# GpSimd in program order, and a step of attention reordered, in a kernel of attention and routed experts

## The chip, the cores and the metric

The kernel runs on one core of a Trainium2 chip, as one launch. The metric is the device time of the launch in microseconds: the median of the runs of the kernel before is 896.27 us (three runs, 895.25 to 897.72).

## The reference

Attention over 8 batches, 12 heads, 448 positions and a head size of 64, with capped scores, then a layer of 8 experts with a fixed capacity:

```
scores = cap*tanh(q@k.T/sqrt(64)/cap);  scores -= max;  attn = exp(scores);  attn /= sum + 1e-9
x = (attn@v) as rows of 768;  logits = x@w_gate
all (token, expert) pairs in order of falling logit: take a pair if the token is free and the expert has under 448 tokens
out[tokens of e] = relu(x@w1[e])@w2[e]
```

All inputs and the output are float32. There are 3584 tokens.

## The kernel before, in words

There are two stages. The first is attention (`attention`); the second routes the tokens and runs the experts (`Routing`, `ffn_all`). Everything that changes is in the first.

**A step.** The loop `for g in range(N)` has 24 steps. Step g takes four heads of one batch: b, m = divmod(g, 3), so a batch has a first, a second and a third step (m = 0, 1, 2). Two pairs of heads lie one above the other in the 128 partitions. In step g the program issues:

- `qk(g,r)`, r = 0 to 6: PE multiplies 64 keys by all queries into a PSUM tile of two banks (psS, two buffers), and ScalarE takes the tanh. After the second, the fourth and the seventh it has a group of tiles together and takes their exponential (line 154). From g = 3 on the first two exponentials are held back by one tanh.
- `avq(g-1,r)`: PE multiplies the values of the step before by its exponentials into two banks named psA. The seven parts are interleaved with those of `qk`.
- `esum`: VectorE adds the exponentials to `es`, for the denominators: e1 (the first two groups, right after the second exponential), and in the next step e2, r6 and in some steps r0.
- `tr(g+1,0)`, `tr(g+1,1)`: VectorE transposes k and q of the next step in blocks of 32.
- `av_out`: VectorE copies psA, one copy for each bank, to `xT`. The tile psA has two buffers of one bank.

**Work for earlier batches.** With bb = b-1, `rnd(bb,..)` multiplies `xT` by the gate weights and `es` by columns of ones on PE. In a third step `logit_in` copies that to SBUF, `sums` transposes the denominators and takes their reciprocals, and GpSimd copies them to `R32`. At the end of the third step `logit` transposes the logits on PE (four matmuls, line 240), scales them on VectorE (lines 245 to 253), and GpSimd adds over heads (line 257). In the first step of every other batch `on_logits` runs `propose_a` on VectorE (twelve small instructions, lines 462 to 473) and `propose_b` on GpSimd. `turn(b-2,p)` handles one pair of the batch two before: VectorE transposes it in blocks (x32, two buffers), GpSimd scales it (`xw`, line 229), and after two of them SP stores the result to `xs` in DRAM (line 233).

**What sets the order.** `manual_schedule` keeps PE, ScalarE, VectorE and SP in the order in which the program is written. GpSimd is not in its list, and a planner orders GpSimd's instructions. Each engine executes its own queue in order. The two PSUM pools here have 2 banks (pM, tiles psM: gate and sum results, logits) and 2 banks (pT, tiles psA); psS has 4.

Of the kernel before, what the change touches and what calls it, by code (L numbers as in the profile page):

```python
# [6 lines left out]
F32=mybir.dt.float32; F32R=mybir.dt.float32r; BF16=mybir.dt.bfloat16; F16=mybir.dt.float16; I32=mybir.dt.int32; I16=mybir.dt.int16  # L7
# [10 lines left out]
def attention(nc, tc, c1, xp, pM, q, k, v, cap, w_gate, xs, L1, ident, on_logits, on_turn, NDEF, setup, mark):  # L18
# [3 lines left out]
    B,H,S,D=q.shape  # L22
    CP=112; NJ=S//CP; NP=H//2; NQ=NP//2; E=w_gate.shape[1]; HG=2
    N=B*NQ
# [20 lines left out]
            if p==NP-1: nc.sync.dma_start(xs[b*S:(b+1)*S].rearrange("(j p) d -> p j d",j=NJ),xn[b])  # L45
        return rest
    with ExitStack() as ctx:
        ctx.enter_context(tc.manual_schedule(engines={mybir.EngineType.PE,mybir.EngineType.Activation,mybir.EngineType.DVE,mybir.EngineType.SP}))
        nat=ctx.enter_context(tc.tile_pool(name="nat",bufs=3))
        tp=ctx.enter_context(tc.tile_pool(name="tp",bufs=2))  # L50
        ep=ctx.enter_context(tc.tile_pool(name="ep",bufs=2))
# [5 lines left out]
        NB=S//32  # L57
# [99 lines left out]
        def esum(g,what):  # L157
# [13 lines left out]
            else:  # L171
                r=int(what[1])
                add(t[:,0],t[:,0],ev(g,r) if r else t[:,1])
        avp={}
        def avq(g,r):
            if not 0<=g<N: return
            if r==0:
                for o in range(2): avp[g,o]=pM.tile([128,512],F32,name="psM") if g==N-1 and not o else pT.tile([128,512],F32,name="psA")
            if g:
                z=nats[g,2]  # L180
                for o in range(2):
                    hp=slice(o*64,o*64+64)
                    for h in range(2):
                        nc.tensor.matmul(avp[g,o][h*64:h*64+64,:S],z[hp,r,h,:],ev(g,r)[hp,h,:],start=r==0,stop=r==6)  # L184
                return
            j,x=(r%3,r//3) if r<6 else (3,1)
            z,zh=nats[g,2]
            for w in range(2):
                o=w^x; hp=slice(w*64,w*64+64)
                for h in range(2):  # L190
                    lhs,rhs=(z[hp,j,HG*h+o,:],ex(g,o,j)) if j<3 else (zh[hp,h,:],ev(g,6))
                    nc.tensor.matmul(avp[g,o][h*64:h*64+64,:S],lhs,rhs[hp,h,:],start=(j==0 and x==0),stop=j==3)
        def av_out(g,o):
            if not 0<=g<N: return
            b,m=divmod(g,NQ)
            if m==0 and o==0: xT[b]=xp.tile([128,NP,S],F32,name="xT",bufs=3)
            nc.vector.tensor_copy(xT[b][:,2*m+o,:],avp[g,o][:,:S])  # L197
        def rnd(b,*ns,of=None):
            of=of or (ROUNDS if b else FIRST)
            for n in ns:  # L200
# [17 lines left out]
            for x in range(4): nc.gpsimd.tensor_copy(R32[b][32*x:32*x+32],rec[64+32*(x//2):96+32*(x//2)])  # L218
        def stored():
            while stores: stores.pop(0)()  # L220
        def turn(b,p):
            stored()
            if not 0<=b<B-NDEF: return
            t=xp.tile([128,S],F32,name="x32",bufs=2)
            nc.vector.transpose(t,xT[b][:,p,:])
            m,o=divmod(p,2); r=(0,2,1,3,4,5)[p]
            if not o: xw[0]=xp.tile([128,NB,32,2],F32,name="xw",bufs=2)
            w=xw[0]
            nc.gpsimd.tensor_tensor(w[:,:,:,o],t.rearrange("p (k i) -> p k i",i=32),R32[b][:,:,r:r+1].broadcast_to([128,NB,32]),op=ALU.mult)
            def store():  # L230
                for x in range(4):
                    c=m*256+x*64
                    nc.sync.dma_start(xs[b*S:(b+1)*S,c:c+64].rearrange("(k q) d -> q k d",q=32),w[32*x:32*x+32].rearrange("p k i o -> p k (i o)"))
            if o: stores.append(store)
        def logit(b,what=0,part=None,pool=None):
            p0=64 if what==2 else 0; W=128-p0
            lg=lgs.pop(b)
            ps=pool.tile([128,512],F32,name="psA") if pool else pM.tile([128,512],F32,name="psM")
            for j in range(NJ):
                mark[0]=nc.tensor.transpose(ps[:CP,j*W:(j+1)*W],lg[p0:,j*CP:(j+1)*CP],ident[p0:,p0:])  # L240
            va=ps[:CP,:NJ*W].rearrange("p (j c) -> p j c",j=NJ)
            if b not in rin: rin[b]=xp.tile([CP,NJ,H],F32,name="rin",bufs=2)
            r=rin[b]
# [10 lines left out]
                    r[:,:,8:12].unsqueeze(3).broadcast_to([CP,NJ,4,E]),op=ALU.mult)  # L254
            if what!=1:
                if b<B-NDEF:
                    add=lambda o,x,y: nc.gpsimd.tensor_tensor(o,x,y,op=ALU.add)
                    add(t[:,:,0:6],t[:,:,0:6],t[:,:,6:12])
                    add(t[:,:,0:3],t[:,:,0:3],t[:,:,3:6])
                    add(t[:,:,0:1],t[:,:,0:1],t[:,:,1:2])  # L260
                    add(L1[:,b*NJ:(b+1)*NJ,:].unsqueeze(2),t[:,:,0:1],t[:,:,2:3])
                else: nc.vector.tensor_reduce(L1[:,b*NJ:(b+1)*NJ,:],t.rearrange("p j s e -> p j e s"),axis=AX.X,op=ALU.add)
# [808 lines left out]
```

## Time and profile before

| what | value |
|---|---|
| median of three runs | 896.27 us |
| profiled execution, its own time | 895.05 us |
| its span | 893.1 us |
| PE busy | 854.5 us, 96% |
| VectorE (DVE) busy | 594.6 us, 67% |
| ScalarE (ACT) busy | 574.5 us, 64% |
| GpSimd (POOL) busy | 418.1 us, 47% |
| mean granted clock of TensorE | 0.994 |

The span is from the first to the last instruction of the program; the execution's own time is 1.95 us longer. A line such as "L149 ACT" names the line of the kernel and the engine. In a timeline the first column is the start in us, the second the duration of the instructions that were merged into the line, xN their number, and the bracket the idle time of the engine before them and what ended it. A PE line counts each matmul of this kernel twice or more, since float32 takes several passes.

### The profile page before, as it was taken

The page shows a single profiled execution, that of the slowest core. Times are in us where ns is not written, and L with a number is a line of the kernel's source. Part 1 is how long each engine was busy: PE and PEld are TensorE (multiplying, and loading weights), DVE is VectorE, ACT ScalarE, POOL GpSimd, SP SyncE. Part 2 cuts the span into 40 slices and gives each one's busy share as a digit, 9 for nine tenths or more (in the row PEclk, how much of TensorE's full clock was granted, in tenths as well). Part 3 has the DMA queues.
Part 4 walks back from the last instruction along what each step waited for, and adds up shares of the span by engine and source line. Part 5 has one row for each costly group of instructions (what it writes and reads, how often), then busy time and mean ns, then how long its engine had stood idle before and what let it go on. Part 6 is the DMA issues. An engine that isn't in the chain of part 4 may idle for free.

```text
span 893.1 us, 17659 instructions
## 1 busy us (share of the span) xinstructions
PE 854.5 (96%) x6092; PEld 621.4 (70%) x6092; DVE 594.6 (67%) x1967; ACT 574.5 (64%) x813; POOL 418.1 (47%) x626
## 2 busy tenths in 40 slices
PE   6999998998999898899999999999999999999997
PEld 3333333333333336888988989989989989999997
DVE  3778887888787988866777777777767773130210
ACT  6899996987989775256374573673754745425521
POOL 8102121213031214356465585593784765856941
PEclk9999999999999999999999999999999999999999
DMA  8899999598885311470760882864936927928701
GB/s 119 131 144 150 156 148 171 98 167 123 141 124 94 70 35 63 150 244 17 226 181 19 232 264 78 239 215 144 275 112 194 280 84 189 312 61 233 240 10 54
DMA packets 363385, 133.70 MB, mean 150 GB/s; under 512 B 290624, under 2 KB 356160, under 8 KB 363296
## 3 DMA queue, kind: packets, MB, share of 16 engines
q1 hardware_dynamic: 353792, 102.27, 54.6%
q0 software_dynamic: 4656, 22.02, 7.2%
q10 hardware_dynamic: 4848, 8.29, 2.9%
q8 instruction: 48, 0.79, 0.4%
q14 instruction: 41, 0.34, 0.1%
HBM read 94.40 MB, written 30.08 MB: 139 GB/s over the span
## 4 chain that ended last, share of the span: by engine, by line
PE 63%; DVE 10%; issue 9%; DMA 5%; SPq 5%; ACT 4%; POOL 4%; POOLq 0%; DVEq 0%; ACTq 0%
PE psH L914 23%; PE psH L945 19%; PE psA L184 9%; PE psS L138 7%; DVE es L160 3%; SPq L85 2%; DMA k<-in_k_dram 2%; ACT e L149 2%; PE psM L206 2%; ACT e L154 2%; DMA xg<-xs,idx 1%; DVE xT L197 1%; DVE cmpD L527 1%; POOL out_dram L927 1%; POOL w2l L796 1%
## 5 line engine op out<-in xcount | busy, mean ns | idle before, releaser
L945 PE MATMUL psH<-w2h,hh 128*128 128x384 f32 x896 | 235.3, 340 | 0.0
L149 ACT ACTIVATE e<-psS 128x896 f32<-128x896 f32 x168 | 148.2, 913 | 39.1 <-PE psS L138 34.5
L945 PE MATMUL psH<-w2l,hh 128*128 128x384 f32 x512 | 166.5, 340 | 0.3 <-POOL gap L794 0.2
L138 PE MATMUL psS<-tq,tk 64*64 64x448 f32 x1288 | 152.0, 549 | 11.1 <-DVE tq L123 5.6
L945 PEld LDWEIGHTS psH<-w2h,hh 128*128 128x128 f32 x896 | 161.8, 188 | 0.3
L184 PE MATMUL psA<-e,nv 64*64 64x448 f32 x1260 | 147.2, 547 | 10.1 <-DVE xT L197 10.1
L154 ACT ACTIVATE e<-e,bias 128x1792 f32<-128x1792 f32 (+2 forms) x74 | 147.2, 1991 | 1.0
L914 PE MATMUL psH<-xgh,w1h 128*128 128x448 f32 x384 | 143.1, 373 | 0.3 <-ACT xgh L874 0.3
L914 PE MATMUL psH<-xgh,w1l 128*128 128x448 f32 x384 | 141.4, 368 | 0.0
L914 PE MATMUL psH<-xgl,w1h 128*128 128x448 f32 x384 | 136.8, 369 | 0.0
L796 POOL TENSOR_TENSOR w2l<-w2r,w2h 128x768 fp32r<-128x768 f32 x64 | 118.1, 1846 | 37.7 <-ACT w2h L792 26.9
L796 POOL TENSOR_TENSOR w1l<-w1r,w1h 128x768 fp32r<-128x768 f32 x62 | 114.3, 1845 | 19.2 <-ACT w1h L792 14.9
L138 PEld LDWEIGHTS psS<-tq,tk 64*64 64x64 f32 x1288 | 50.1, 133 | 92.7 <-issue 45.4
L184 PEld LDWEIGHTS psA<-e,nv 64*64 64x64 f32 x1260 | 53.4, 135 | 80.7 <-issue 55.6
L945 PEld LDWEIGHTS psH<-w2l,hh 128*128 128x128 f32 x512 | 95.6, 188 | 1.3 <-POOL gap L794 1.2
L920 ACT ACTIVATE hh<-psH 128x448 fp32r<-128x448 f32 x64 | 34.8, 544 | 86.1 <-PE psH L914 79.8
L922 DVE SCALAR_TENSOR_TENSOR hh<-psH,hh 128x64 fp32r<-128x64 f32 (+1 forms) x128 | 43.9, 385 | 67.4 <-ACT hh L920 66.3
L951 ACT ACTIVATE on<-psH 128x384 f32<-128x384 f32 x48 | 23.4, 487 | 88.5 <-PE psH L945 82.5
L160 DVE TENSOR_TENSOR es<-es,e 128x896 f32<-128x896 f32 (+2 forms) x51 | 77.2, 1513 | 1.4 <-ACT e L154 0.3
L914 PEld LDWEIGHTS psH<-xgh,w1h 128*128 128x128 f32 x384 | 72.5, 189 | 5.6 <-ACT xgh L874 0.5
L914 PEld LDWEIGHTS psH<-xgh,w1l 128*128 128x128 f32 x384 | 72.3, 188 | 5.2
L914 PEld LDWEIGHTS psH<-xgl,w1h 128*128 128x128 f32 x384 | 72.2, 189 | 5.0
(368 smaller groups left out, 1269.2 us busy)
## 6 DMA issues: line engine op xcount, KB each, us to landing
w1r<-in_moe_w_dram SPq DMA_DIRECT2D x128, 192.0 KB, 4.6
w2r<-in_moe_w_dram SPq DMA_DIRECT2D x64, 384.0 KB, 6.0
k<-in_k_dram SPq DMA_DIRECT2D x92, 112.0 KB, 3.8
q<-in_q_dram SPq DMA_DIRECT2D x92, 112.0 KB, 4.0
nv<-in_v_dram SPq DMA_DIRECT2D x92, 112.0 KB, 3.2
xs<-xw SPq DMA_DIRECT2D x72, 112.0 KB, 2.5
xz<-pl ACTq DMA_DIRECT2D x18, 384.0 KB, 3.1
xs<-xn SPq DMA_DIRECT2D x2, 1344.0 KB, 6.2
```

The lines of the kernel that those rows point to most:

```text
L85: (nc.scalar if first and a else nc.sync).dma_start(z[w:w+32,lo*NB:hi*NB,:],src[b,h0+2*t+lo:h0+2*t+hi,:,a*32:a*32+32].rearrange("h (k s) d ...
L138: nc.tensor.matmul(ps[o*64:o*64+64,h,:S],tks[g,0][hp,o,r*64:r*64+64],tks[g,1][hp,o,:],start=True,stop=True)
L149: nc.scalar.activation(ev(g,r),ps[:,:,:S],AF.Tanh,scale=sr[0])
L154: act=lambda: nc.scalar.activation(e,e,AF.Exp,scale=sr[1],bias=bias)
L160: t=es_t[g]; add=lambda o,a,b: nc.vector.tensor_tensor(o,a,b,op=ALU.add)
L184: nc.tensor.matmul(avp[g,o][h*64:h*64+64,:S],z[hp,r,h,:],ev(g,r)[hp,h,:],start=r==0,stop=r==6)
L796: (eng or nc.gpsimd).tensor_tensor(view(l),r,view(h).bitcast(F32),op=ALU.subtract)
L914: nc.tensor.matmul(ps[:,:C],a[:,c,:],b[:,c,:],start=(m==0),stop=(m==DC*3-1)); m+=1
L920: nc.scalar.activation(h[:,:C],ps[:,:C],AF.Relu)
L922: nc.vector.scalar_tensor_tensor(h[:,d:d+b-a],ps[:,a:b],0.0,h[:,a:b].bitcast(F32),op0=ALU.max,op1=ALU.subtract)
L945: nc.tensor.matmul(ps[:,:HD],h[:,f,a:a+128],spl[p,2,hf,f//2][w][:,f%2,:],start=(m==0),stop=(m==nm-1))
L951: if t<3: nc.scalar.activation(ons[p][0][:,t*DM+hf*HD:t*DM+hf*HD+HD],ps[:,:HD],AF.Copy)
```

## The change

1. GpSimd is added to the list of `manual_schedule`: its instructions run in program order.
2. psA becomes one tile of two banks with one buffer. `av_out(g)` is one copy of both banks, and it is issued at the start of step g+2, ahead of the first `avq`, and no longer at the end of step g+1. The last step keeps two tiles (`alast`) and two copies.
3. `turn(b,m)` takes both pairs of a step in one transpose and one scaling (x32 with one buffer of twice the size), at the start of the step, behind `av_out` and `heads` and ahead of both block transposes `tr`. Before there were two, at two places in the step.
4. From g = 3 on both block transposes stand together ahead of `esum`.
5. `logit` is split: `ltr` (PE's transposes) in the middle of the next first step, the rest at the end of that step, the sums over heads (`heads`, GpSimd) at the start of the second step, `on_logits` at the end of the second step.
6. `logit_in` and `sums` go from the middle of the third step to its end, behind e1. In the last third step (g = 23) `logit_in` and `logit` stay in the middle.

```diff
-        ctx.enter_context(tc.manual_schedule(engines={mybir.EngineType.PE,mybir.EngineType.Activation,mybir.EngineType.DVE,mybir.EngineType.SP}))
+        ctx.enter_context(tc.manual_schedule(engines={mybir.EngineType.PE,mybir.EngineType.Activation,mybir.EngineType.DVE,mybir.EngineType.Pool,mybir.EngineType.SP}))
...
+                two=None if g==N-1 else pT.tile([128,2,512],F32,name="psA",bufs=1)
+                for o in range(2): avp[g,o]=(alast(o) if two is None else two[:,o])
+                pair[0]=two
...
+            if g<N-1: nc.vector.tensor_copy(xT[b][:,2*m:2*m+2,:],pair[0][:,:,:S])
+            else:
+                for o in range(2): nc.vector.tensor_copy(xT[b][:,2*m+o,:],avp[g,o][:,:S])
...
+        def turn(b,m):
             if not 0<=b<B-NDEF: return
+            t=xp.tile([128,2,S],F32,name="x32",bufs=1)
+            nc.vector.transpose(t.rearrange("p o s -> p (o s)"),xT[b][:,2*m:2*m+2,:].rearrange("p o s -> p (o s)"))
+            w=xp.tile([128,NB,32,2],F32,name="xw",bufs=2)
+            r=R32[b][:,:,m:m+3:2] if m<2 else R32[b][:,:,4:6]
+            nc.gpsimd.tensor_tensor(w.rearrange("p k i o -> p k o i"),t.rearrange("p o (k i) -> p k o i",i=32),r.unsqueeze(3).broadcast_to([128,NB,2,32]),op=ALU.mult)
...
+        def heads(b):
+            if b not in lts: return
+            t=lts.pop(b)
+            add=lambda o,x,y: nc.gpsimd.tensor_tensor(o,x,y,op=ALU.add)
+            add(t[:,:,0:6],t[:,:,0:6],t[:,:,6:12])
+            add(t[:,:,0:3],t[:,:,0:3],t[:,:,3:6])
+            add(t[:,:,0:1],t[:,:,0:1],t[:,:,1:2])
+            add(L1[:,b*NJ:(b+1)*NJ,:].unsqueeze(2),t[:,:,0:1],t[:,:,2:3])
...
             order=g>=G2; first=bb==0
+            av_out(g-2)
+            if m==0 and bb>1: on_turn(bb-2)
             for j in range(2 if order else 3): avq(g-1,j)
-            turn(b-2,2*m)
+            stored()
+            if m==1: heads(bb-1)
+            turn(b-2,m)
             tr(g+1,0)
+            if order: tr(g+1,1)
             for w in ('e2','r') if g==1 else ('e2','r6','r0'): esum(g-1,w)
             qk(g,2)
             if order: avq(g-1,2)
             if m==2 and bb>=0: rnd(bb,3)
             qk(g,3)
             if order: qk(g,4)
-            if m==0 and bb>1: on_turn(bb-2)
+            if m==0 and 0<=bb-1<B-NDEF: ltr(bb-1)
             if m==0 and bb>=0: rnd(bb,*((0,1) if first else (0,)))
             if m==1 and bb>=0: rnd(bb,*((2,) if first else (1,2)))
-            if m==0 and bb>0: on_logits(bb-1)
-            if m==2 and bb>=0:
-                logit_in(bb)
-                if bb<B-NDEF: sums(bb)
-                else: logit(bb)
-            turn(b-2,2*m+1)
-            tr(g+1,1)
+            if b==B-1 and m==2: logit_in(bb); logit(bb)
+            if not order: tr(g+1,1)
             if order: qk(g,5)
             else: qk(g,4)
             avq(g-1,3); avq(g-1,4)
...
             avq(g-1,6)
             esum(g,'e1')
-            if g: av_out(g-1,0); av_out(g-1,1)
-            if m==2 and 0<=bb<B-NDEF: logit(bb)
+            if m==0 and 0<=bb-1<B-NDEF: logit(bb-1)
+            if m==1 and bb>0: on_logits(bb-1)
+            if m==2 and 0<=bb<B-NDEF: logit_in(bb); sums(bb)
+        av_out(N-2)
         stored()
```

## Rows read from the trace of the kernel before

**Rows 1.** Busy time in stretches of the attention stage. Columns: stretch, its length, then busy us (and instructions) of PE, PEld, DVE, ACT and POOL, the granted clock of PE, the share of DMA and GB/s.

```profile
124.42:142.62 18.20, 14.19 (x126) 5.06 (x122) 17.67 (x26) 11.88 (x11) 5.62 (x12) 0.91 1.10 156
86.98:305.54 218.56, 202.84 (x1989) 76.98 (x1985) 182.99 (x228) 188.86 (x161) 49.32 (x95) 0.98 0.84 133
...
138.00:141.00 3.00, 3.00 (x18) 1.29 (x22) 3.00 (x4) 0.00 (x0) 0.96 (x1) 0.55 1.50 152
...
302.40:306.00 3.60, 3.53 (x36) 2.33 (x38) 3.60 (x5) 0.46 (x1) 0.97 (x1) 1.00 0.30 66
```

**Rows 2.** Timeline of ScalarE (ACT): tanh is line 149, the exponential line 154. Each row but the one at 92.75 is the third tanh of a step (the steps 5, 6, 7, 9, 10 and 22); 92.75 is the sixth and seventh of step 6.

```profile
74.15 0.92 ACT L149 ACTIVATE e<-psS 128x896 f32<-128x896 f32 x1 [0.29 <-PE psS L138]
...
86.98 0.92 ACT L149 ACTIVATE e<-psS 128x896 f32<-128x896 f32 x1 [0.91 <-PE psS L138]
...
92.75 1.91 ACT L149 ACTIVATE e<-psS 128x896 f32<-128x896 f32 x2
...
99.13 0.92 ACT L149 ACTIVATE e<-psS 128x896 f32<-128x896 f32 x1 [0.29 <-PE psS L138]
...
124.42 0.92 ACT L149 ACTIVATE e<-psS 128x896 f32<-128x896 f32 x1 [0.91 <-PE psS L138]
...
142.62 0.92 ACT L149 ACTIVATE e<-psS 128x896 f32<-128x896 f32 x1 [5.93 <-PE psS L138]
...
305.54 0.92 ACT L149 ACTIVATE e<-psS 128x896 f32<-128x896 f32 x1 [4.36 <-PE psS L138]
```

**Rows 3.** Timeline of VectorE (DVE), from steps 6, 8 and 9. L160 is `esum`, L210 and L216 are `logit_in` and `sums`, L225 the transpose of a pair, L123 that of q, L245 to L253 `logit`, L462 the first of `propose_a`, L197 `av_out`.

```profile
92.91 2.03 DVE L160 TENSOR_TENSOR es<-e,e 128x1792 f32<-128x1792 f32 x1 [0.22 <-ACT e L154]
...
113.32 0.62 DVE L210 COPY lg<-psM 128x448 f32<-128x448 f32 x1
...
116.00 0.65 DVE L225 STREAM_TRANSPOSE x<-xT 128x448 f32<-128x448 f32 x1
116.57 1.07 DVE L123 STREAM_TRANSPOSE tq<-q 128x896 f32<-128x896 f32 x1
...
120.96 0.35 DVE L245 RECIPROCAL rin<-psM 112x32 f32<-112x32 f32 x1
...
121.68 0.28 DVE L253 TENSOR_TENSOR lt<-psM,rin 112x128 f32<-112x128 f32 x1
124.78 0.65 DVE L225 STREAM_TRANSPOSE x<-xT 128x448 f32<-128x448 f32 x1 [2.82 <-POOL xw L229]
...
130.49 0.21 DVE L462 TENSOR_REDUCE r_m<-L 112x8 f32<-112x64 f32 x1
...
132.14 0.64 DVE L225 STREAM_TRANSPOSE x<-xT 128x448 f32<-128x448 f32 x1
...
133.69 3.70 DVE L160 TENSOR_TENSOR es<-e,e 128x1792 f32<-128x1792 f32 x1
137.31 1.14 DVE L197 COPY xT<-psA 128x448 f32<-128x448 f32 x2
```

**Rows 4.** Timeline of GpSimd (POOL): L257 is the sum over heads, L229 the scaling of a pair.

```profile
122.11 1.38 POOL L257 TENSOR_TENSOR lt<-lt 112x192 f32<-112x192 f32 x3 [4.87 <-DVE lt L253]
...
133.62 1.89 POOL L229 TENSOR_TENSOR xw<-x,R 128x448 f32<-128x448 f32 x2
...
327.79 2.65 POOL L229 TENSOR_TENSOR xw<-x,R 128x448 f32<-128x448 f32 x1 [10.96 <-DVE x L225]
```

**Rows 5.** The chain of waits up to 120 us, in order of time: start, us, what (merged). L184 is `avq`, L206 `rnd`, L240 the transposes of `logit`.

```profile
82.42 0.58 PE psM L240 x4
...
96.68 1.50 PE psA L184 x16
...
101.32 1.64 PE psM L206 x16
...
109.14 1.50 PE psA L184 x16
```

**Rows 6.** Timeline of PE, the first `avq` of the steps 10 and 22.

```profile
137.98 3.04 PE L184 MATMUL psA<-e,nv 64*64 64x448 f32 x14 [2.33 <-DVE xT L197]
...
302.47 1.88 PE L184 MATMUL psA<-e,nv 64*64 64x448 f32 x14 [2.33 <-DVE xT L197]
```

**Rows 7.** Timelines of the start: two rows of GpSimd in `setup` (a mask, the iota of line 398), three of VectorE, and the third tanh of step 3 on ScalarE.

```profile
2.92 0.54 POOL L368 TENSOR_SCALAR r_lo<-r_ii 112x112 f16<-112x112 int32 x1
...
6.90 0.16 POOL L398 IOTA r_qi<- 128x32 int32 x1
...
10.64 0.18 DVE L364 TENSOR_SCALAR r_jj<-r_ii 128x128 int32<-128x128 int32 x1
...
17.00 1.11 DVE L123 STREAM_TRANSPOSE tq<-q 128x896 f32<-128x896 f32 x1 [2.34 <-DMA q<-in_q_dram]
...
37.71 1.11 DVE L123 STREAM_TRANSPOSE tk<-k 128x896 f32<-128x896 f32 x1 [4.12 <-DMA k<-in_k_dram]
...
49.56 0.92 ACT L149 ACTIVATE e<-psS 128x896 f32<-128x896 f32 x1 [1.34 <-PE psS L138]
```

**Rows 8.** The chain of waits near the end of attention, in order of time: e2 of step 22.

```profile
316.12 2.60 DVE es L160
```

**Rows 9.** The instructions on tile q after 60 us: duration min/median/max in ns, first and last start in us.

```profile
L85 SPq DMA_DIRECT2D q<-in_q_dram x72: 311/701/2433, 61.8 to 273.0; - x72
L123 DVE STREAM_TRANSPOSE tq<-q x19: 1068/1070/1111, 63.2 to 309.2; 128x896 f32<-128x896 f32 x19
```

More of the change, by code (lines that the diff above doesn't have):

```diff
@@ L173, in esum, with alast @@
                 add(t[:,0],t[:,0],ev(g,r) if r else t[:,1])
-        avp={}
+        avp={}; tl=[]; pair=[None]
+        def alast(o):
+            if not o: return pM.tile([128,512],F32,name="psM")
+            tl.append(pT.tile([128,2,512],F32,name="psA",bufs=1))
+            return tl[0][:,0]
         def avq(g,r):
@@ L177, in avq @@
             if r==0:
-                for o in range(2): avp[g,o]=pM.tile([128,512],F32,name="psM") if g==N-1 and not o else pT.tile([128,512],F32,name="psA")
+                two=None if g==N-1 else pT.tile([128,2,512],F32,name="psA",bufs=1)
+                for o in range(2): avp[g,o]=(alast(o) if two is None else two[:,o])
+                pair[0]=two
             if g:
@@ L192, in avq, with av_out @@
                     nc.tensor.matmul(avp[g,o][h*64:h*64+64,:S],lhs,rhs[hp,h,:],start=(j==0 and x==0),stop=j==3)
-        def av_out(g,o):
+        def av_out(g):
             if not 0<=g<N: return
             b,m=divmod(g,NQ)
-            if m==0 and o==0: xT[b]=xp.tile([128,NP,S],F32,name="xT",bufs=3)
-            nc.vector.tensor_copy(xT[b][:,2*m+o,:],avp[g,o][:,:S])
+            if m==0: xT[b]=xp.tile([128,NP,S],F32,name="xT",bufs=3)
+            if g<N-1: nc.vector.tensor_copy(xT[b][:,2*m:2*m+2,:],pair[0][:,:,:S])
+            else:
+                for o in range(2): nc.vector.tensor_copy(xT[b][:,2*m+o,:],avp[g,o][:,:S])
         def rnd(b,*ns,of=None):
@@ L220, in stored @@
             while stores: stores.pop(0)()
-        def turn(b,p):
-            stored()
+        def turn(b,m):
             if not 0<=b<B-NDEF: return
[L224 to L229, printed above, removed]
+            t=xp.tile([128,2,S],F32,name="x32",bufs=1)
[3 more added lines that the diff above has]
+            nc.gpsimd.tensor_tensor(w.rearrange("p k i o -> p k o i"),t.rearrange("p o (k i) -> p k o i",i=32),r.unsqueeze(3).broadcast_to([128,NB,2,32]),op=ALU.mult)
             def store():
@@ L233, in store, with ltr @@
                     nc.sync.dma_start(xs[b*S:(b+1)*S,c:c+64].rearrange("(k q) d -> q k d",q=32),w[32*x:32*x+32].rearrange("p k i o -> p k (i o)"))
-            if o: stores.append(store)
+            stores.append(store)
+        lps={}
+        def ltr(b,what=0,pool=None):
+            p0=64 if what==2 else 0; W=128-p0
+            lg=lgs.pop(b)
+            ps=tl[0][:,1] if pool else pM.tile([128,512],F32,name="psM")
+            for j in range(NJ):
+                mark[0]=nc.tensor.transpose(ps[:CP,j*W:(j+1)*W],lg[p0:,j*CP:(j+1)*CP],ident[p0:,p0:])
+            lps[b]=ps
+        lts={}
         def logit(b,what=0,part=None,pool=None):
             p0=64 if what==2 else 0; W=128-p0
[L237 to L240, printed above, removed]
+            if b not in lps: ltr(b,what,pool)
+            ps=lps.pop(b)
             va=ps[:CP,:NJ*W].rearrange("p (j c) -> p j c",j=NJ)
@@ L256, in logit @@
                 if b<B-NDEF:
[L257 to L262, printed above, removed]
+                    lts[b]=t
+                    return
+                nc.vector.tensor_reduce(L1[:,b*NJ:(b+1)*NJ,:],t.rearrange("p j s e -> p j e s"),axis=AX.X,op=ALU.add)
                 if b>=B-2: on_logits(b)
@@ L334, in attention @@
         for r in range(3,7): avq(g,r)
-        av_out(g,0); av_out(g,1)
+        av_out(g)
         LAST=[RC,RD]
```

## The prediction, as put on record before the run

> **What bounds the kernel now.** The table of busy time says PE 96% over the whole span, but that is an average over stages. The change touches only attention, up to about 340 us, so I cut that stage out. Over sixteen steps of it (86.98 to 305.54 us) ScalarE is busy 188.86 of 218.56 us, PE 202.84, VectorE 182.99, GpSimd 49.32 [rows 1]. None is full, and PE's busy time contains its pauses between parts of a group, so I looked for what a step waits for.
>
> I use one marker: the start of the third tanh of a step ("t2", on `qk(g,2)`), because ScalarE stops there every time. From 86.98 to 124.42, three steps without a disturbance take 37.44 us; the first of them takes 12.15 (86.98 to 99.13) and the third of the batch before 12.83 (74.15 to 86.98), so the second takes 37.44 - 12.15 - 12.83 = 12.46 [rows 2]. Five such batches and one first step would be 5 x 37.44 + 12.15 = 199.35 us, but 86.98 to 305.54 took 218.56. So 19.2 us are lost, and the rows say where: t2 at 142.62 waited 5.93 us and t2 at 305.54 waited 4.36 us for PE, both after a first step (g = 9 and g = 21).
>
> The cause is VectorE's queue [rows 3]. At the start of step 9 the transpose at 124.78 waits 2.82 us for GpSimd, whose planner put the head sums of 122.11 ahead of the scalings [rows 4]. Then `propose_a` takes 130.49 to 132.14 (1.65 us). Then the sum at 133.69 takes 3.70 us where the same sum at 92.91 took 2.03: two scalings run on GpSimd from 133.62 for 1.89 us [rows 4]. So the copies of `av_out` come at 137.31, and `avq` of the next step has no free PSUM buffer: PE stands 2.33 us until 137.98 [rows 6].
>
> **What the change removes.** (a) Scaling now follows one transpose of both pairs and runs under the transposes of k and q; transposes did not grow beside GpSimd (0.64 at 132.14 beside `propose_b`, 0.65 at 116.00 without the scaling [rows 3]), and the sum comes after them. (b) The transpose has its own turn of the single x32 buffer a whole step after the last scaling, so the 2.82 us wait goes. (c) `propose_a` leaves the first step for the end of the second. (d) Four PE transposes (0.58 us [rows 5]) leave the boundary between third and first step, where they made the third step 12.83 and not about 12.2; they go to the middle of the first step.
>
> **What it adds.** `av_out` of step g was right behind the sum e1 on VectorE and still is, but now something is queued between them: in a first step the logit's four instructions, in a second step of every other batch `propose_a`, in a third step `logit_in` and `sums`. These stood before where VectorE had time (113.32 to 116.00, ahead of e1), or behind `av_out` (120.96). Behind the copy waits `avq(g,0)` of the next step, behind that `qk(g+1,2)`, behind that t2. I follow this chain from t2 to t2:
>
> - t2 to the sixth tanh, which starts when the second exponential ends: 92.75 - 86.98 = 5.77 [rows 2].
> - e1 starts 0.16 later (92.91); it holds VectorE 2.03, and the next instruction starts 0.08 before its end (133.69 + 3.70 = 137.39 against 137.31): 1.95 [rows 3].
> - the work put between, E: logit 120.96 to 121.68 + 0.28 = 1.00; `propose_a` 1.65; `logit_in` and `sums` 113.32 to 116.00 = 2.68 [rows 3].
> - one copy of two banks. No row shows it. Two copies take 1.14 together (137.31), so one is about 0.62 with the 0.08 overlap. A transpose goes from 0.65 (448 columns) to 1.07 (896) [rows 3], which adds 0.42: lower end 1.04. Upper end 1.23, two copies without overlap. I take 1.08, near the transposes, since it is one instruction of their size.
> - copy end to t2: PE starts 0.05 later (137.31 + 0.62 = 137.93 against 137.98), and from `avq`'s start 96.68 to t2 at 99.13 are 2.45 [rows 2, 5, 6]. Together 2.50; I take 2.55, since PE now begins from a stand.
>
> Sum without E: 5.77 + 0.16 + 1.95 + 1.08 + 2.55 = 11.51.
> First step: 11.51 + 1.00 = 12.51. PE alone would need 12.46 - 0.82 + 0.58 = 12.22 (12.46 is 96.68 to 109.14, a second step in which PE never stops; half of its sixteen sums and gates of 1.64 us go, the transposes come [rows 5]), so the copy decides by a little.
> Second step: 11.51 is less than PE's 12.46, so 12.46; with `propose_a` 11.51 + 1.65 = 13.16.
> Third step: 11.51 + 2.68 = 14.19 against 12.83 now. This is the price of the change: PE is through with its queue about 9.6 us after t2 (12.46 less the 2.45 of the last `avq` and `qk`, less half the sums, plus about 0.4 of waiting for ScalarE), the copy ends 8.96 + 2.68 = 11.64 after it, so PE stands about 2.0 us.
>
> **Sum.** Third step 5 is 14.19. Steps 6 to 20 are five batches; `propose_a` falls into steps 10, 16 and 22. Three batches of 12.51 + 12.46 + 14.19 = 39.16 and two of 39.86 are 197.20; step 21 is 12.51. From t2 at 74.15 to t2 of step 22: 223.90, now 231.39: -7.5 us. In parts: the stalls give -19.2, first steps cost 6 x 0.36 = +2.2, third steps 6 x 1.36 = +8.2, `propose_a` 2 x 0.70 = +1.4.
>
> **Tail.** The sum of step 22 now starts at 316.12, when ScalarE is done, 10.58 after t2. Afterwards it is queued behind `propose_a`, copy and a turn of 1.00 with nothing of k or q to cover it: 5.77 + 0.16 + 1.95 + 1.65 + 1.08 + 1.00 = 11.61, 1.0 later. It then takes 1.95 and not 2.60 (a scaling runs beside it in the trace [rows 8]), and the second transpose of a single pair (0.64 less 0.08 of overlap, as at 132.14 [rows 3]) is gone: -0.2 at the last copy but one. PE's first `avq` of the last step can no longer start after half a copy, about +0.45 (half of 1.08, less overlap). Together +0.25.
>
> **Start.** GpSimd in program order holds at the first mask in `setup` (line 366), which needs VectorE's instruction at 10.64; the planner ran it after all the iotas. What stands from 2.92 to 7.06 (4.1 us) then comes after 10.82, with that mask (about 0.6, like the one at 2.92), a wait for VectorE and two more masks (about 1.3) before the last iota that VectorE needs (line 398): about 16.9, so the transpose of q at 17.00 ends at about 19.2 and not 18.1 [rows 7]. The steps begin 1.1 us late. It costs nothing as long as VectorE's wait for k (4.12 us, to 37.71) and what follows it set t2 of step 3, which has 1.34 us of waiting at 49.56 [rows 7]. If that cover is gone, it costs 1.1.
>
> Elsewhere nothing moves: SP still gets the loads of a step and then the stores of the step before; k and q wait for the same transposes, now earlier; `heads` runs on GpSimd under copy and turn. I put these at zero, since SP runs steps ahead: it issued the last load of q at 273.0, VectorE transposed the last q at 309.2 [rows 9].
>
> Total -7.25, say -7.3. The profiled execution took 895.05 (span 893.1) and so comes to 887.7; the median of the runs is 896.27, 1.2 above it, and comes to **889.0**.
>
> **Rivals.**
> *The clock falls in the new waits.* [...] t2 at 142.62 came 4.17 after the copies' end (137.31 + 1.14); with 2.55 it would have come 1.6 earlier. The new wait of 2.0 is a little shorter than both; a fall in one place and none in the other, after the same wait, leave it open: 14%. Six third steps: 6 x 1.6 = +9.6, so 898.6, no change. [...]
>
> *GpSimd's scaling outlasts the two turns (slower).* It starts about 2.2 after the copy starts, and k and q cover it until 4.05. The sums behind it need 3.0, in first steps 4.0, and e1 is due at 1.08 + 2.55 + 5.77 + 0.16 = 9.56. So it may last 3.4 us in first steps and 4.4 in others before it decides. From 133.62 two scalings take 1.89; the last one, at 327.79, took 2.65 beside a sum [rows 4]. At 2 x 2.65 = 5.3 each first step loses 1.9, each third step and each with `propose_a` 0.9: 6 x 1.9 + 6 x 0.9 + 3 x 0.9 = 19.5, so 908.5. Against it: the scalings without a sum beside them need 0.95 each. 5%. [...]
>
> *The third step's extra work is hidden after all*, because e1 could start earlier than I think: then 6 x 1.36 is not paid and the time is 880.8. Against it: e1 needs the second exponential, and at 92.91 it already waits for it. 6%.
>
> **How the numbers follow.** The forecast holds with 61%: 885 to 893.5 (each of fifteen bound steps 0.15 shorter or longer is 2.3 us; the start 1.1). The other 14% are mishaps that no row names, a third for each sign. About 0.3%, or 2.7 us, is what can be told from no change: faster is below 893.6, slower above 899.0. Faster: 0.61 + 0.06 + 0.04 = 0.71; same: 0.14 + 0.05 = 0.19; slower: 0.05 + 0.05 = 0.10. The range from 884 to 899 takes in the clock rival and leaves out the hidden work, the long scaling and part of the rest.
>
> **What would show it.** t2 no longer waits 4 to 6 us after first steps. Steps measure about 12.5, 12.5 (13.2 with `propose_a`) and 14.2. Between e1 and the copy of 1.08 us on VectorE stand the named pieces, and PE waits about 2 us for that copy at the start of each batch, at full clock. Sums no longer take 3.70. Wrong it would be with a granted clock below 1 there, with a scaling still running when e2 starts, or with t2 of step 3 later than 49.6.

## The result, and the profile after

The changed kernel takes **900.71 us** (median of eight runs, 896.98 to 901.73) against 894.97 for the kernel before on the same chip (eight runs, 893.95 to 897.72): a ratio of 1.0055, 95% interval 1.0036 to 1.0073. It is slower by about 0.6%; 889.0 was forecast, and 900.71 is outside the range. The profiled execution took 900.15 us (span 898.2, mean granted clock 0.988); 887.7 was forecast for it.

I cut both spans at the third tanh ("t2") of the steps 5 and 22 and at the first gather (GpSimd's indirect load of `xg`) of the second stage. The third stretch is called the tail below.

| us | before | forecast | after |
|---|---|---|---|
| start to t2 of step 5 | 74.15 | 74.15 | 74.39 |
| t2 of step 5 to t2 of step 22 | 231.39 | 223.90 | 230.87 |
| t2 of step 22 to the first gather | 68.81 | 69.06 | 72.08 |
| first gather to the end of the span | 518.75 | 518.75 | 520.86 |

Of the 7.5 us that the steps were to give, 0.5 came; the tail and the second stage took 5.4 more. The timeline of ScalarE after shows where, its bracket the wait ahead of each t2 (first steps 6, 9, 12, 15, 18, 21, then steps 22 and 23):

```profile
88.70 0.92 ACT L149 ACTIVATE e<-psS 128x896 f32<-128x896 f32 x1 [2.39 <-PE psS L138]
...
129.39 0.92 ACT L149 ACTIVATE e<-psS 128x896 f32<-128x896 f32 x1 [3.84 <-PE psS L138]
...
171.13 0.92 ACT L149 ACTIVATE e<-psS 128x896 f32<-128x896 f32 x1 [4.09 <-PE psS L138]
...
212.06 0.92 ACT L149 ACTIVATE e<-psS 128x896 f32<-128x896 f32 x1 [4.08 <-PE psS L138]
...
252.04 0.92 ACT L149 ACTIVATE e<-psS 128x896 f32<-128x896 f32 x1 [2.39 <-PE psS L138]
...
292.23 0.92 ACT L149 ACTIVATE e<-psS 128x896 f32<-128x896 f32 x1 [3.34 <-PE psS L138]
...
305.26 0.92 ACT L149 ACTIVATE e<-psS 128x896 f32<-128x896 f32 x1 [0.29 <-PE psS L138]
...
318.45 0.92 ACT L149 ACTIVATE e<-psS 128x896 f32<-128x896 f32 x1 [1.03 <-PE psS L138]
```

The waits of 5.93 and 4.36 after first steps [rows 2] are gone (0.29 at 305.26). In their place each third step ends with a wait: 2.39 twice, 3.34 to 4.09 four times. VectorE at the first of the long ones (L218 to L224 are `logit_in` and `sums`, L203 the copy, L232 the turn):

```profile
119.61 2.03 DVE L160 TENSOR_TENSOR es<-e,e 128x1792 f32<-128x1792 f32 x1 [2.75 <-ACT e L154]
121.56 0.62 DVE L218 COPY lg<-psM 128x448 f32<-128x448 f32 x1
122.21 0.62 DVE L220 TENSOR_TENSOR lg<-lg,psM 64x448 f32<-64x448 f32 x1
122.86 0.64 DVE L223 STREAM_TRANSPOSE lgt<-lg 64x448 f32<-64x448 f32 x1
123.54 0.68 DVE L224 RECIPROCAL rec<-lgt 64x84 f32<-64x84 f32 x1
124.24 1.09 DVE L203 COPY xT<-psA 128x896 f32<-128x896 f32 x1
125.36 1.11 DVE L232 STREAM_TRANSPOSE x<-xT 128x896 f32<-128x896 f32 x1
126.40 1.07 DVE L123 STREAM_TRANSPOSE tk<-k 128x896 f32<-128x896 f32 x1
127.39 1.07 DVE L123 STREAM_TRANSPOSE tq<-q 128x896 f32<-128x896 f32 x1
128.39 3.11 DVE L160 TENSOR_TENSOR es<-es,e 128x1792 f32<-128x1792 f32 x2
```

This queue is the one that was forecast: 2.68 us between e1 and the copy, the copy 1.09. VectorE waited 2.75 for ScalarE ahead of e1, so that work had a free place. PE's timeline, at the first and the second of these boundaries:

```profile
86.15 1.73 PE L190 MATMUL psA<-e,nv 64*64 64x448 f32 x16 [1.99 <-DVE xT L203]
...
125.39 2.45 PE L190 MATMUL psA<-e,nv 64*64 64x448 f32 x16 [2.00 <-DVE xT L203]
127.59 1.74 PE L138 MATMUL psS<-tq,tk 64*64 64x448 f32 x8
```

And the table of stretches behind the six waits (columns as in [rows 1]; the third number from the right is PE's granted clock):

```profile
86.00:88.70 2.70, 2.55 (x28) 1.13 (x32) 2.67 (x4) 0.31 (x1) 1.46 (x2) 1.00 0.96 178
126.00:129.40 3.40, 3.40 (x24) 1.25 (x20) 3.40 (x4) 0.01 (x1) 1.73 (x1) 0.54 1.36 183
168.00:171.20 3.20, 3.20 (x24) 1.23 (x20) 3.20 (x3) 0.07 (x1) 1.72 (x1) 0.59 0.42 68
209.00:212.10 3.10, 3.10 (x24) 1.21 (x20) 3.10 (x3) 0.04 (x1) 1.73 (x1) 0.58 0.41 65
249.00:252.10 3.10, 2.61 (x28) 1.13 (x32) 3.07 (x5) 0.71 (x2) 1.72 (x3) 1.00 0.20 46
288.00:292.30 4.30, 3.57 (x28) 1.47 (x32) 4.27 (x5) 0.96 (x3) 2.45 (x4) 0.75 0.00 0
```

The wait is nearly the same at all six, 2.0 us (1.84 at the fifth). After two of them the granted clock stayed at 1.00; after four it was 0.54 to 0.75, and at the second boundary the sixteen PE records of `avq` took 2.45 us and not the 1.73 of the first. The third steps 8, 11, 14 and 20 lasted 15.76, 16.01, 16.00 and 15.26 where steps 5 and 17 lasted 14.31 and 14.32.

### The profile page after: what moved, and what is told of

The parts are those of the page before. It is cut to its first block, busy times and chain, and to the rows that moved or that the text cites. A ratio compares the mean times of both kernels' runs of the same rounds, so it can differ in the third digit from the quotient of the medians.

```text
span 898.2 us, 17569 instructions
## 1 busy us (share of the span) xinstructions
PE 856.6 (95%) x6092; PEld 615.4 (69%) x6092; DVE 586.0 (65%) x1926; ACT 574.4 (64%) x813; POOL 420.9 (47%) x608
## 4 chain that ended last, share of the span: by engine, by line
PE 59%; DVE 11%; issue 10%; SPq 6%; ACT 6%; DMA 5%; POOL 3%; POOLq 0%; DVEq 0%
PE psH L934 22%; PE psH L965 19%; PE psA L190 7%; PE psS L138 6%; SPq L85 4%; DVE es L160 3%; ACT e L149 3%; ACT e L154 2%; DVE xT L203 2%; DMA xs<-xw 1%; PE psM L214 1%; SPq L239 1%; DVE cmpD L547 1%; POOL xg L841 1%; POOL w2l L816 1%
## 5 line engine op out<-in xcount | busy, mean ns | idle before, releaser
L190 PE MATMUL psA<-e,nv 64*64 64x448 f32 x1260 | 143.6, 557 | 14.6 <-DVE xT L203 13.7
L138 PE MATMUL psS<-tq,tk 64*64 64x448 f32 x1288 | 148.1, 556 | 7.2 <-ACT e L149 4.7
L190 PEld LDWEIGHTS psA<-e,nv 64*64 64x64 f32 x1260 | 48.5, 137 | 93.2 <-issue 63.6
L138 PEld LDWEIGHTS psS<-tq,tk 64*64 64x64 f32 x1288 | 46.4, 135 | 92.3 <-issue 50.6
L160 DVE TENSOR_TENSOR es<-e,e 128x1792 f32<-128x1792 f32 (+1 forms) x24 | 47.5, 1981 | 49.0 <-ACT e L154 49.0
L160 DVE TENSOR_TENSOR es<-es,e 128x896 f32<-128x896 f32 (+2 forms) x51 | 76.6, 1503 | 1.1
```

The costliest lines, as they stand in the source:

```text
L138: nc.tensor.matmul(ps[o*64:o*64+64,h,:S],tks[g,0][hp,o,r*64:r*64+64],tks[g,1][hp,o,:],start=True,stop=True)
L160: t=es_t[g]; add=lambda o,a,b: nc.vector.tensor_tensor(o,a,b,op=ALU.add)
```

## The experiments

Each is compared with the kernel before on the same chip in the same session (medians 895.55 to 895.9; 894.97 beside the change itself, so a comparison across sessions carries about 1 us of that). The stretches are those of above, from one profiled execution of each kernel, in us:

| kernel | median us | to t2 of step 5 | steps 5 to 22 | tail | second stage |
|---|---|---|---|---|---|
| before | 894.97 | 74.15 | 231.39 | 68.81 | 518.75 |
| after | 900.71 | 74.39 | 230.87 | 72.08 | 520.86 |
| e1, PE kept busy | 892.78 | 74.15 | 224.42 | 71.76 | 519.97 |
| e2, sums in the middle | 881.08 | 75.64 | 212.11 | 71.44 | 519.91 |
| e3, copy first | 881.88 | 75.93 | 211.53 | 74.16 | 519.98 |
| e4, before + GpSimd's order | 879.62 | 74.86 | 214.93 | 68.78 | 518.93 |
| e5, tail | 896.06 | 74.71 | 230.87 | 68.72 | 520.30 |
| e6, order of `setup` | 897.56 | 73.43 | 230.69 | 72.20 | 519.38 |
| e7 = e2 + e3 | 881.69 | 74.08 | 211.99 | 72.80 | 520.63 |
| e8 = e7 + e5 + e6 | 876.96 | 74.06 | 211.99 | 68.96 | 519.99 |
| e9 = e8 + `propose_a` moved | 874.10 | 73.13 | 209.49 | 68.62 | 520.86 |
| e10 = e4 + part 5 | 876.49 | 74.41 | 210.27 | 69.62 | 520.20 |

**e1: the same waits of VectorE, but PE kept busy.** In first steps from step 6 on PE computes `qk(g,1)` three times, with the same numbers.

```diff
+              for _ in range(3 if r==1 and g>5 and g%NQ==0 else 1):
```

> The changed kernel, but PE repeats the second part of qk twice in each first step from step 6 on (same numbers, 2 x 0.75 us of work in the wait for the copy). Theory 1 (the clock): the waits of about 2 us before each batch are VectorE's, and in four of six of them TensorE's clock falls, which costs another 1.0 to 1.7 us each. Then with PE busy the granted clock stays at 1.00 at these places, all six third steps measure 14.2 to 14.4 us instead of up to 16.0, and the time falls by about 6 us to about 895. Rival (the long waits have another cause, and the clock only follows them): third steps still of 15.3 to 16.0 us, 901 or more.

Measured: 892.78, ratio 0.997 (0.9956 to 0.9983), 8 us under the change as it is and 2 under what was expected. PE's timeline at step 6, then ScalarE's at steps 6, 9, 12 and 21 (lines are one higher):

```profile
85.91 1.73 PE L191 MATMUL psA<-e,nv 64*64 64x448 f32 x16 [0.49 <-DVE xT L204]
```

```profile
88.47 0.92 ACT L150 ACTIVATE e<-psS 128x896 f32<-128x896 f32 x1 [2.06 <-PE psS L139]
...
127.70 0.92 ACT L150 ACTIVATE e<-psS 128x896 f32<-128x896 f32 x1 [2.06 <-PE psS L139]
...
167.67 0.92 ACT L150 ACTIVATE e<-psS 128x896 f32<-128x896 f32 x1 [2.06 <-PE psS L139]
...
286.11 0.92 ACT L150 ACTIVATE e<-psS 128x896 f32<-128x896 f32 x1 [2.05 <-PE psS L139]
```

PE stands 0.49 here and 0.48 at step 21 (283.55), instead of 2.0; the granted clock is 1.00 behind all six boundaries, and all six third steps last 14.31 or 14.32. More work for PE made the kernel faster. The steps 5 to 22 took 224.42 against 230.87, so the falls had cost 6.45 us, and 224.42 is the 223.90 of the forecast but for 0.5.

**e2 and e3: the wait itself taken away, in two ways.** e2 puts `logit_in` and `sums` back into the middle of the third step; e3 leaves them and puts the copy right behind e1, ahead of them.

```diff
+            if m==2 and bb>=0:
+                logit_in(bb)
+                if bb<B-NDEF: sums(bb)
+                else: logit(bb)
...
-            if m==2 and 0<=bb<B-NDEF: logit_in(bb); sums(bb)
```

```diff
-            av_out(g-2)
...
             esum(g,'e1')
+            av_out(g-1)
```

> The changed kernel, but logit_in and sums go back to the middle of the third step, ahead of e1. Theory 1 (the work between e1 and the copy is what the change costs): third steps of 12.2 to 12.6 us instead of 14.3 to 16.0, no fall of the clock there, about 18 us less, about 883. Rival (VectorE is short of time in the third step wherever the 2.7 us stand): e1 comes later by them, third steps of 13.5 us and more, less than half of that gain, 892 or more.

> The changed kernel, but the one copy stands right behind e1 at the end of each step, and logit, propose_a, logit_in and sums follow it. Theory 1: third steps of 12.2 to 12.5 us, second steps of 12.5 us with and without propose_a; in first steps the 2.7 us push e1 about 1.2 us past the second exponential, 12.6 to 12.8 us. About 18 us less, about 883. Rival (the work only moves the lateness on to the next step): first steps of 14 us and more, 890 or more.

Measured: 881.08 (0.9838, 0.9818 to 0.9858) and 881.88 (0.9836, 0.982 to 0.9853), both 1 to 2 us under what was expected. ScalarE at t2 of the steps 5 and 6 in e2, where the third step 5 takes 12.22 and its wait is gone:

```profile
75.64 0.92 ACT L149 ACTIVATE e<-psS 128x896 f32<-128x896 f32 x1 [0.29 <-PE psS L138]
...
87.86 0.92 ACT L149 ACTIVATE e<-psS 128x896 f32<-128x896 f32 x1 [0.29 <-PE psS L138]
```

Third steps last 12.22 to 12.41 in e2 and 12.22 to 12.23 (once 12.70) in e3. Against 14.31 that is 2.1 us six times, and the 6.45 of the clock go with it. In e3 the tail is 2.1 longer than after. The trace shows `propose_a` behind the copy of step 22 in VectorE's queue, ahead of the turn and the sums; the last logits come 18.1 after t2 of step 22 (305.53) and not 17.1 (322.35 after), and PE stands 3.79 us for them, at a clock of 0.57 from 305 to 310:

```profile
306.94 1.07 PE L247 MATMUL psM<-ident,lg 128*112 128x128 f32 x4 [3.79 <-DVE lg L220]
```

**e4: of the change only part 1.** The kernel before, with GpSimd in program order.

```diff
-mybir.EngineType.DVE,mybir.EngineType.SP}))
+mybir.EngineType.DVE,mybir.EngineType.Pool,mybir.EngineType.SP}))
```

> The kernel before with GpSimd in program order and nothing else of the change. Theory 1 (the stalls of the kernel before start with the planner's order, which put the sums over heads ahead of a scaling that VectorE waits for): VectorE's wait of 2.82 us at the start of first steps goes, the waits of 4.4 to 5.9 us after first steps with propose_a fall to 1 to 2.5 us, those of 1.6 to 1.8 us to under 0.5; about 12 to 15 us less than before, 880 to 883. Rival (the stalls come from propose_a and from sums shut out by scalings, whatever GpSimd's order): under 5 us less, 890 or more.

Measured: 879.62, ratio 0.9813 (0.9797 to 0.983). One name in a list makes the kernel 16 us faster, a little more than the 12 to 15 that were expected. GpSimd's timeline at the place of [rows 4], then VectorE's at the place of [rows 3]:

```profile
118.05 0.97 POOL L229 TENSOR_TENSOR xw<-x,R 128x448 f32<-128x448 f32 x1
122.97 1.40 POOL L257 TENSOR_TENSOR lt<-lt 112x192 f32<-112x192 f32 x3 [3.95 <-DVE lt L253]
124.45 2.01 POOL L257 TENSOR_TENSOR L<-lt 112x32 f32<-112x32 f32 x1
126.41 0.97 POOL L229 TENSOR_TENSOR xw<-x,R 128x448 f32<-128x448 f32 x1
```

```profile
122.80 0.64 DVE L225 STREAM_TRANSPOSE x<-xT 128x448 f32<-128x448 f32 x1
...
132.57 1.98 DVE L160 TENSOR_TENSOR es<-e,e 128x1792 f32<-128x1792 f32 x1
134.48 1.14 DVE L197 COPY xT<-psA 128x448 f32<-128x448 f32 x2
```

The scaling runs at 118.05, ahead of the head sums and not behind them, so the transpose at 122.80 waits for nothing (2.82 before), two scalings no longer pile up beside e1 (1.98, before 3.70), and the copies start 9.35 after t2 of step 9 (125.13) and not 12.89. Steps 9, 15 and 21 take 13.07 instead of 18.20, 18.04 and 16.63, steps 12 and 18 take 12.15 instead of 13.47 and 13.64: together the 16.46 us by which steps 5 to 22 are shorter. So 16.5 of the 19.2 us of stalls that the forecast put down to four edits together go with part 1 alone.

**e5: the tail.** The last logits take a PSUM bank of psS instead of the second half of the tile that the last `avq` writes, and the last turn goes behind `logit_in`.

```diff
-            ps=tl[0][:,1] if pool else pM.tile([128,512],F32,name="psM")
+            ps=pS.tile([128,2,512],F32,name="psS")[:,0] if pool else pM.tile([128,512],F32,name="psM")
...
-            turn(b-2,m)
+            if g<N-1: turn(b-2,m)
...
-            if b==B-1 and m==2: logit_in(bb); logit(bb)
+            if b==B-1 and m==2: logit_in(bb); turn(b-2,m); logit(bb)
```

> The changed kernel, but with two edits in its last step: the last logits are transposed into a bank of psS, not into the second bank of the last psA tile, and the last turn stands behind logit_in, not ahead of e2. Theory 2 (the end of attention is longer because the last scaling shuts out e2 and r6, and because the last avq waits for VectorE's reading of the same tile): e2 and r6 take 3.1 us together instead of 4.5, PE's wait of 0.5 us for lt goes, and from t2 of step 23 to the first gather 55.5 to 56.8 us pass instead of 58.9 (56.4 in the kernel before); about 2 to 3 us less, about 898. Rival (the end is longer because the clock falls there, and those two do not matter): 58 us and more.

Measured: 896.06 (0.9987, 0.9972 to 1.0003). The tail is 68.72, 3.4 shorter than after. VectorE and GpSimd after, then PE after, then VectorE and GpSimd in e5:

```profile
316.79 4.51 DVE L160 TENSOR_TENSOR es<-es,e 128x1792 f32<-128x1792 f32 x2
...
316.94 3.41 POOL L235 TENSOR_TENSOR xw<-x,R 128x896 f32<-128x896 f32 x1 [0.32 <-DVE x L232]
```

```profile
323.76 0.62 PE L247 MATMUL psM<-ident,lg 128*112 128x128 f32 x4 [2.07 <-DVE lg L220]
337.44 0.59 PE L190 MATMUL psA<-e,nv 64*64 64x448 f32 x2 [0.53 <-DVE lt L262]
```

```profile
316.16 3.19 DVE L160 TENSOR_TENSOR es<-es,e 128x1792 f32<-128x1792 f32 x2
...
322.92 1.72 POOL L235 TENSOR_TENSOR xw<-x,R 128x896 f32<-128x896 f32 x1 [3.51 <-DVE x L232]
```

After, the last scaling and two sums share the same 4.5 us, and both grow (1.72 to 3.41, 3.19 to 4.51). The two sums apart, e2 and r6:

```profile
316.79 1.98 DVE L160 TENSOR_TENSOR es<-es,e 128x1792 f32<-128x1792 f32 x1
...
318.81 2.50 DVE L160 TENSOR_TENSOR es<-es,e 128x896 f32<-128x896 f32 x1
```

e2 doesn't grow; the scaling, begun 0.15 later, lasts past its end, and r6 behind it takes 2.50. PE then stands 2.07 for the logits, and the clock from 325.5 to 328 is 0.57. In e5 scaling and sums don't meet and the clock from 324 to 328 is 1.00. The 0.53 at 337.44 is PE waiting until VectorE has read logits that lie in the other bank of the same tile; it is gone too. From t2 of step 23 to the first gather 55.53 us pass, as expected. The run doesn't separate the three causes, but e1 bounds one of them: there r6 takes 2.50 as after, ScalarE's last two tanhs wait for PE not at all and 0.26 where they wait 0.81 and 1.12 after, and the tail is 71.76. So I put the low clock at about 0.3 of the 3.4 (72.08 less 71.76), an estimate from one profile of each.

**e6: the start.** Four masks of GpSimd go to the end of `setup`.

```diff
-        nc.gpsimd.tensor_scalar(s.bo,jj,0.0,None,op0=ALU.is_equal)
...
         for n in ("VA","q"): nc.gpsimd.memset(s.V[n][:,s.NV:],-1.0)
+        nc.gpsimd.tensor_scalar(s.bo,jj,0.0,None,op0=ALU.is_equal)
```

> The changed kernel, but the four masks of setup that need VectorE stand at its end. Theory 3 (GpSimd in program order holds at the first mask and delays VectorE at the start): t2 of step 1 comes at 24.6 to 25.0 us instead of 26.0; t2 of step 3 at 49.5 to 49.8 as now, so the time changes by less than 0.5 us. Rival (the delay at the start is carried on): t2 of step 3 earlier by 1 us and the time with it.

Measured: 897.56 (1.0018, 1.0001 to 1.0035), 3 us under the change where less than 0.5 was expected. The start is 1.0 shorter than after, and the second stage of this profile 1.5. t2 of step 3, expected at 49.5 to 49.8 as after (49.79), comes at 48.83: by this sign the rival holds, and the delay at the start is carried on. The transposes of k and q, at 17.30 and 18.33 after, are back at 13.80 and 17.33. But the starts of the kernels without this edit spread from 74.08 to 75.93, so one profile doesn't settle 1 us; the kernels with it have 73.13 to 74.06.

**e7 and e8: the edits together.**

> The edits of e2 and e3 together: logit_in and sums in the middle of the third step, the copy right behind e1, logit and propose_a behind the copy. Theory 1: no step has anything between e1 and the copy, and none has more than VectorE can do before e1: first steps 12.2 to 12.5 us, second 12.5, third 12.2; about 1 to 2 us less than either alone, 879 to 880.5. Rival (the two edits give the same gain once, and the work behind the copy makes e1 late again): 881 or more.

> The edits of e2, e3, e5 and e6 together. The theories together: steps as in e7, the end of attention 2 to 3 us shorter than there, the start up to 1.5 us shorter: 875 to 877, below the kernel before with GpSimd in program order alone (879.6). Rival (what the end or the start gains is given back in the routing, which waits for something else): 879 or more.

Measured: 881.69 (0.9836, 0.9817 to 0.9854) and 876.96 (0.9785, 0.9765 to 0.9805). e8 is as expected; e7 is not, its rival holds (the work behind the copy makes e1 late again). With the copy first *and* the sums in the middle, first steps measure 12.28, second 12.45 and third 12.22, but the third steps 11 and 17 take 13.6: `propose_a`, behind the copy of step 10, moves VectorE's queue of step 11 back until e1 is late, and t2 waits 1.66 (the row is from e8):

```profile
161.56 0.92 ACT L149 ACTIVATE e<-psS 128x896 f32<-128x896 f32 x1 [1.66 <-PE psS L138]
```

PE stands 1.26 us there and 1.08 in step 17, and the granted clock stays at 1.00.

**e9: `propose_a` in the middle of the second step. e10: e4 and of the change only part 5**, with `propose_a` at that same place.

```diff
+            if m==1 and bb>0: on_logits(bb-1)
             if not order: tr(g+1,1)
...
-            if m==1 and bb>0: on_logits(bb-1)
```

> The kernel of e8_all, with propose_a issued in the middle of the second step, ahead of the third transposes and of e1, and no longer behind the copy at its end. In e8_all the third steps that follow propose_a (11 and 17) took 13.59 and 13.56 instead of 12.22, and t2 behind them waited 1.65. Theory (VectorE's own queue: propose_a behind the copy of step 10 moves the turn, the transposes and e2 of step 11 back by 1.65, and with logit_in and sums in the middle of that step e1 comes late): in a second step VectorE waits 1.3 us for ScalarE ahead of e1, and the copy has 0.95 to spare besides, so propose_a fits there at no cost; steps 11 and 17 take 12.22, the last step begins with less in VectorE's queue, and the time is 2.7 to 4.5 under e8_all (876.96): 872.5 to 874.3. Rival (the wait at 161.56 is a wait for ScalarE or for a transfer, which propose_a only marks): 876.5 to 877.5, with 13.6 at steps 11 and 17 as before.

> The kernel before with GpSimd in program order (e4_pool_only, 879.62), and of the change only part 5 besides: logits a step later, with PE's transposes in the middle of the first step, the scaling at its end behind the copies, the sums over heads at the start of the second step, propose_a in the middle of the second step. Copies, turns and block transposes stay as before. Theory (what is left in e4_pool_only are 0.6 us of PE's transposes at six boundaries of third and first step and 0.92 in each of three first steps with propose_a): third steps 12.2 to 12.3, first steps 12.15 to 12.3, second 12.46, so 5 to 6.5 us under e4_pool_only: 873 to 874.7. Rival (the single scalings of GpSimd beside the sums, and turns of one pair each, cost as much in the middle of the steps once nothing else binds, so the one turn for two pairs and the one copy are needed as well): no third or first step under 12.5, 877 to 880.

Measured: 874.10 (0.9746, 0.9722 to 0.9771), as expected, and 876.49 (0.9774, 0.9747 to 0.98). In e9 the wait at 161.56 is gone, and steps 11 and 17 take 12.22 and 12.41:

```profile
159.27 0.92 ACT L149 ACTIVATE e<-psS 128x896 f32<-128x896 f32 x1 [0.29 <-PE psS L138]
```

PE is now busy in all but 1.7 us of the steps (stretch from t2 of step 5 to t2 of step 22):

```profile
73.13:282.62 209.49, 207.78 (x2109) 74.72 (x2105) 185.80 (x197) 200.36 (x171) 57.56 (x79) 1.00 0.99 148
```

e9 is 2.5% faster than the kernel before and the best of all. e10 is 1.8 us above the upper end that its theory gave, but its steps are as expected (first 12.28, second 12.46, third 12.22 to 12.32): 210.27, only 0.8 more than e9. So one copy, one turn for two pairs and the block transposes moved together (parts 2 to 4) are worth at most about 1 us in the steps, as far as one profile of each tells. What misses lies in step 18 (12.96), in step 22 (13.47, where t2 then waits 1.31) and in the start; the causes stay open.

## Why the prediction was wrong

**Right.** The stall and its cause: the planner had put the head sums ahead of the scalings, shown by e4 and its rows. The chain from t2 to t2: first steps without a fall just before 12.47 (12.51 forecast), second 12.46, with `propose_a` 13.20 and 13.19 (13.16), third 14.31 where the clock held (14.19). The copy at 1.08 to 1.09, the wait of PE at 2.0, sums of 2.03 and no longer 3.70. The delay at the start: q's transpose ended at 19.4 (19.2 forecast) and t2 of step 1 came 1.3 late (1.1).

**Right by luck: that it costs nothing.** t2 of step 3 came only 0.2 late, but not because VectorE's wait for k covered it: that k came at 36.24 and not at 37.71, and t2 of step 3 then waited 0.29 and not 1.34. Without the delay (e6) k came at 36.58 and t2 of step 3 at 48.83, so the delay was carried on: from t2 of step 1 to t2 of step 3 pass 23.75 with it and without it. The kernel before needs 24.81, 1.06 more, behind its later k; why that k came earlier in all the others was not tried.

**The step that failed: PE's new waits counted "at full clock".** The sum has no term for the clock; its fall stands only as a rival, at 14%, and the note on it was that a fall in one place and none in the other, after the same wait, leave it open: two waits of 2.33 us [rows 6], with a clock of 0.55 behind the first and 1.00 behind the second [rows 1]. That is no ground for 14%: read as it stands, it says half of the waits fall. And the kernel before has a third stand of 2.33 us, behind step 15, which the prediction left out; there the clock fell too. PE, and the stretch behind it:

```profile
220.22 3.66 PE L184 MATMUL psA<-e,nv 64*64 64x448 f32 x16 [2.33 <-DVE xT L197]
```

```profile
222.00:224.00 2.00, 2.00 (x16) 1.14 (x12) 2.00 (x2) 0.00 (x0) 0.30 (x1) 0.59 0.95 193
```

So it was two of three before. After, it was four of six, at 1.45, 1.70, 1.69 and 0.95 us, about the 1.6 that the rival took. With what followed in the next steps this is 6.45 us (e1), half of the miss. That the wait was "a little shorter" was no ground either: 2.00 against 2.33 made no difference. This term alone gives 889.0 + 6.45 = 895.5, inside the range; the next two, put at 0.25 and at nothing, carried the time out of it.

**The tail, mis-sized: +0.25 forecast, +3.3 measured.** e2 started 11.53 after t2 of step 22 (11.61 forecast). It then took 1.98, as forecast (1.95 and not 2.60). What the term left out is r6 behind it: the scaling of two pairs starts 0.15 after e2 and lasts past its end, r6 took 2.50 instead of 1.09, and so the two sums took 4.51 instead of 3.71. In other steps the transposes of k and q stand between turn and sums; in the last step there are none. I had seen that nothing covers the turn there, and not that nothing keeps the scaling from the sums. PE's stand of 2.07, the low clock after it (about 0.3) and the wait within one PSUM tile came on top.

**The long scaling** came true in that one place only: elsewhere it took 1.72 to 1.74 and was over before the sums, if only by about 0.1 us, and far under the 3.4 from which, by the estimate, it decides. That estimate lets the sums begin only when the scaling has ended; for it the rows have one case, the sum of 3.70, which is 1.75 more than 1.95, nearly all of the 1.89 of both scalings.

**The second stage, +2.1, was not foreseen** ("Elsewhere nothing moves"). It is 518.75 and 518.93 in the kernel before and e4, 519.38 to 520.86 in all others. In the two profiles 1.5 us of it stand at one gather. Before, ScalarE has its data at 742.69, 3.95 after the gather's issue at 738.74; after, the issue is at 742.10 and the data is there 5.41 later:

```profile
747.51 1.49 ACT L864 ACTIVATE pl<-xg 128x1536 int16<-128x1536 int16 x1 [2.46 <-DMA xg<-xs,idx]
```

But in e1 the same data was there 3.87 after the issue (735.42 to 739.29), and its second stage is 519.97 all the same. So it accounts for this profile and not for the difference; what does stays open.

The four parts are 0.24 (start), 6.97 (steps: 6.45 of clock, 0.5 of third steps at 14.31), 3.02 (tail) and 2.11: 12.3 of the 12.45 by which the profiled execution missed.

**What the sum didn't ask.** "What the change removes" names four edits (a to d) for one stall of 19.2 us, and asks of none whether it does it alone. e4 answers: the order does 16.5 of it. The rest of the change then costs 21 us (900.71 against 879.62). The largest part is the work of 2.68 between e1 and the copy: e2 and e3 each take back 18.8 to 19.3 us of the steps. I had the price of a third step right and set it against 12.83; against the 12.22 that part 5 makes possible it is 2.1 six times, and the clock.

## What to carry to other kernels

Before a reordering is costed as a whole, cost its smallest part that removes the stall: here one engine's program order did most of what six edits were meant to do (16 us), and two of the others, the copy behind the third step's work and that work at its end, cost more than it gave (18.8 to 19.3 us). Whatever is queued between the last sum and the copy that frees an accumulator is paid once per group by PE, beyond what PE's own work covers; put it where its engine waits for another (ahead of e1, or in the middle of a second step). And where a new wait of PE is about as long as some in the trace, count all of those, and charge the fall of the clock to the same share of the new ones: two of three before, four of six after.

## What the runs showed of the hardware

- Behind the six waits of third steps (after: PE stood 1.84 to 2.0 us) PE was granted a lower clock in some places and not in others, in the same kernel: 0.54 to 0.75 behind four and 1.00 behind two in the profile of after, 0.58 to 0.64 behind four and 1.00 behind two in e5, 0.50 to 0.61 behind four and 1.00 behind two in e6, and not the same four. Behind the stand of 2.07 before the last logits it was 0.57 after (325.5 to 328). After 1.26 and 1.08 us (e8) and at all six places of e1 (0.49 at the first, 0.48 at the last) it stayed at 1.00. What decides at 2 us stays open. The runs of e5, with such waits, go from 892.61 (mean clock 0.994) to 897.90 (0.988); those of e9, without them, from 873.31 to 874.54 (0.998 in all).
- One scaling of two pairs takes 1.72 to 1.74 with no sum beside it, less than two of one pair (1.89 [rows 4]). Begun 0.15 after e2 it took 3.41 while e2 kept its 1.98, and r6, next in VectorE's queue, took 2.50. In e4 a tiny sum of GpSimd (112x32) took 2.01 at 124.45, beside e2; before it took 0.25 at 123.57, with no sum beside it. Transposes and copies of VectorE didn't grow beside a scaling (1.07 at 126.40 and 127.39 after, the two copies of 1.14 at 134.48 in e4, while one ran).
- Two banks in one PSUM tile are one thing to the waits of this program: PE waited 0.53 for a read in the other bank, and in e5, with the logits in another tile, it did not.
